# A sequence mixer and MLP on one core: transposes moved from TensorE to the DMA queue, part of the LayerNorm statistics from VectorE to ScalarE, and a new order of the tasks

## The chip, the core and the metric

One core of a Trainium2 chip runs the whole kernel in one launch. The metric is the device time of one execution in microseconds. Four runs of the kernel before gave 243.87, 244.04, 244.14 and 245.66, with a median of 244.09.

## What is computed

The inputs are bf16: `S` = 2048 rows of `D` = 512, and an MLP width of `F` = 1792. Cut to what matters:

```python
def A(q, k, v, shift_k, ssm_k, ssm_D):           # q is the LayerNorm of x = A_q
    k_shift = sum(k_pad[t:t+S] * shift_k[:, 3-t] for t in range(4))
    kv = k_shift * v
    y = causal_convolution(kv, ssm_k)             # by an FFT of length 2S
    return q * (y + kv * ssm_D)

def B(x, w1, w2, w3, w4):
    h  = gelu(layernorm(x) @ w1)
    hs = concat(h quarters shifted by -1, +1, -2, +2 rows) @ w2
    x1 = x + hs
    return x1 + gelu(layernorm(x1) @ w3) @ w4

h  = x + A(layernorm(x), ...)
h2 = h + B(layernorm(h), ...)
```

## The kernel before

The 2048 rows are held as 16 blocks of 128 rows by 512 columns, and most of the second half works on pairs of blocks (256 rows).

In the first half the long convolution is done as a discrete Fourier transform in two matmul steps each way. The names in the trace follow the steps: `nt` are transposes of k (L352), `pk` the short convolution (L371), `ph` and `pc` the first step for the filter and for the gated input (L326), `pg` and `pw` the second step (L404), `pv` the inverse second step (L490), and matmuls of L565 the inverse first step (tasks J and I, for four blocks at a time). Between the steps ScalarE (ACT) and VectorE (DVE) convert each PSUM tile to bf16 (`copy`, L265 on ACT and L267 on DVE), and DMAs on SP's queue rearrange it across partitions. The last of these DMAs is `ra<-rb` (L495), on which I waits. Two small groups of warm-up matmuls (`warm`, L509 to L512, 4 matmuls each) stand between the last inverse step and J; each waits for one of the last two conversions.

The second half goes block by block. A gate (L576, ACT, task Y) scales the inverse's PSUM tile into z. `hsum` (L585, DVE, task H) forms h from it, and `stats` takes its mean and variance by a bn_stats and a bn_aggr (L582, L583). For each pair `hvar` (DVE), `hnorm` (GpSimd, called POOL in the profile, with a power at L607) and `hbf` (any of three engines, L625 or L627, task hb) give the normalised bf16 block. `transposes` (L635 to L639) sends its four 128x128 tiles through TensorE (PE) by an identity matrix, and `tcopy` brings them from PSUM into `hnT`. Then follow `w1mm` (L653, task W(p, h): two for each pair), a gelu on ACT (L659, task U(p, h)), `w2mm` (L678, task X(b)), which reads the gelus of three neighbouring pairs because of the row shifts, `x1sum` on DVE (L683, task S, with its own `stats`), again a normalisation (`lbf`, task lb), four transposes and a copy into `lnT`, `w3mm` (L720, task M(g, f): 7 for each of 8 pairs), a gelu (L726), and `w4mm` (L735, task O(g, i): 14 matmuls for each of 16 blocks). `store` (L743, task Z) adds the residual and sends the block out on SP's queue; its tile has three buffers. Warm-up matmuls of L751 (4 for each of blocks 2 to 5) are strewn in; block 4's stands last of all PE work, behind the last O.

Which task is issued when is not left to a scheduler: `ORDER` is a list written out by hand or by a planner, of task numbers with the engine's letter (P for PE, A for ACT, V for DVE, G for POOL, D for a DMA on SP's queue). Each engine runs its tasks in this order, and SP's queue, which waits for a DMA's inputs before it issues it, does so too. The tasks' `opts` and `lat` are a planner's costs in microseconds; they no longer act at run time.

Of the kernel before, what the change touches and what calls it, by code (L numbers as in the profile page):

```python
# [34 lines left out]
7D 1D 2D 12G 69P 3D 67P 70A 68V 30P 4D 28P 31A 34P 29V 43P 6D 35A 37P 13G 44A 52P 38V 5D 48P 53A 46P 49V 0D 55P 47A 39P  # L35
41P 40V 56A 8D 65P 42A 66V 61P 59P 62V 63P 60V 57P 10D 64A 71P 58A 18G 14V 32P 75P 33A 9D 72V 25P 76V 19P 26A 79P 36D
276V 20A 277V 15A 21P 283V 73P 80V 22A 16V 23P 77P 74V 24A 280V 27D 89P 278V 50P 90A 83P 78V 51A 11D 297A 103P 84V 105P
81P 104A 281V 106A 275V 101P 82V 85P 279G 102A 282V 45D 111P 86V 284G 113P 112A 99P 100V 114A 125P 17G 123P 54D 126A
127P 124V 93P 128A 129P 94V 117P 130A 115P 108D 118A 91P 116V 131D 87P 92A 132D 137P 88V 141P 119D 138A 135P 107D 142V
139P 95D 136V 140A 97D 143P 157P 110D 144V 158V 153P 120D 147P 154A 134D 149P 148V 179P 121D 150A 151P 133D 180A 191P  # L40
152V 109D 185P 192A 96D 159P 181V 98D 173P 186A 155P 122D 160V 174A 182P 187V 156A 197P 161P 183A 193V 163P 198A 184D
188P 162V 164A 194P 199V 189A 203P 165P 204A 195V 209P 166A 205V 196D 200P 210A 215P 201A 206P 211V 216A 221P 202D 207V
167P 222A 190D 212P 217V 168A 208D 227P 175P 213A 223V 171P 228A 218P 176V 172A 233P 229V 219A 224P 214D 234A 239P 225V
220D 230P 240A 245P 235V 226D 231A 177P 169P 241V 246A 232D 236P 170A 251P 237V 178A 247V 252A 238D 242P 257P 253V 243A
248P 258A 263P 249V 254P 264A 244D 269P 259V 255A 250D 299D 270A 265V 260P 298D 271V 261A 266P 256D 285V 267A 272P 262D
288V 268D 295P 273A 291V 145P 290V 274D 296P 146A 292V 293V 303P 286V 294G 301D 287V 304P 305A 302G 289G 322A 306V 307A
325A 341P 308V 342P 323V 343A 309V 344V 362A 324P 310G 346A 326V 312G 379P 311G 315G 363V 313P 364A 380P 314A 316P 327P
400A 328V 347V 398A 329G 300D 317A 318P 349V 331G 365V 381A 334A 350G 348P 319A 366V 332P 399V 383A 335P 367G 355A 415P
401V 333A 369G 416P 372A 356P 320P 351G 336A 402V 368G 357V 417A 352V 373P 403G 370P 382V 419A 337P 374A 339P 371A 404G
# [12 lines left out]
679P 688A 660A 675P 682V 680A 673P 676A 631P 674A 681V 647P 632A 657P 648A 653P 658A 655P 654A 649P 656A 645P 650A 685P
646V 663P 686V 683P 664V 665P 684V 643P 666V 703P 644V 705P 704V 345P 706V
# [27 lines left out]
def kernel(  # L91
# [417 lines left out]
    def warm(e):  # L509
        pt = big(("wm",))  # L510
        for i in range(4):
            nc.tensor.matmul(pt[:, i % 2, :], lhsT=wup[:, 0:P], rhs=wup[:], start=True, stop=True)  # L512
# [71 lines left out]

    def hsum(b):  # L585
        def f(e):
            nc.vector.scalar_tensor_tensor(out=h_sb[:, b, :], in0=q_sb[:, b, :], scalar=qmv[:, b, 0:1], in1=tl["z", b][:],  # L587
                                           op0=SUB, op1=MUL)
            stats("hv", b, h_sb[:, b, :])
        return f  # L590
# [163 lines left out]
    for b in range(NB):  # L754
# [5 lines left out]
        if 1 < b < 6:  # L760
            task(("wm", b), {"PE": 0.87}, warm(b), [("H", b)], take="mm", rank=-100)
# [65 lines left out]
```

## Time and profile before

| | us |
|---|---|
| median of four runs | 244.09 |
| the profiled execution | 243.03 |
| its span, first to last instruction | 241.2 |
| PE busy | 222.3 (92%) |
| DVE busy | 158.3 (66%) |
| ACT busy | 135.6 (56%) |
| POOL busy | 53.2 (22%) |

A busy share is a mean over stages with different limits, so the stretches and the chain of waits say more than this table. In the rows of a group, the numbers behind the bar are its busy time, the mean duration of one in nanoseconds, and the idle time of the engine just before them with what ended it. Instructions of one engine overlap at their ends, so a dense run of them advances by busy time over count, a little less than the mean.

### The profile page before, as it was taken

The page shows a single profiled execution, that of the slowest core. Times are in us where ns is not written, and L with a number is a line of the kernel's source. Part 1 is how long each engine was busy: PE and PEld are TensorE (multiplying, and loading weights), DVE is VectorE, ACT ScalarE, POOL GpSimd, SP SyncE. Part 2 cuts the span into 40 slices and gives each one's busy share as a digit, 9 for nine tenths or more (in the row PEclk, how much of TensorE's full clock was granted, in tenths as well). Part 3 has the DMA queues.
Part 4 walks back from the last instruction along what each step waited for, and adds up shares of the span by engine and source line. Part 5 has one row for each costly group of instructions (what it writes and reads, how often), then busy time and mean ns, then how long its engine had stood idle before and what let it go on. Part 6 is the DMA issues. An engine that isn't in the chain of part 4 may idle for free.

```text
span 241.2 us, 4733 instructions
## 1 busy us (share of the span) xinstructions
PE 222.3 (92%) x1885; PEld 133.4 (55%) x1905; DVE 158.3 (66%) x324; ACT 135.6 (56%) x195; POOL 53.2 (22%) x102
## 2 busy tenths in 40 slices
PE   7879999798989956699999999999999999999995
PEld 3455454543332313369658757976565769864442
DVE  6686978999989969999998685147391253002221
ACT  3775697899999825689664333653014526730000
POOL 3760025000000052998715070001030000000000
PEclk9999999999999999799999999999999999999999
DMA  6998299881433999000000001000001000001111
GB/s 164 401 422 359 107 287 394 329 332 48 174 132 130 313 323 366 6 1 3 0 3 1 0 3 43 3 1 0 24 22 43 24 22 0 3 0 43 46 43 43
DMA packets 11816, 28.10 MB, mean 116 GB/s; under 512 B 1809, under 2 KB 6674, under 8 KB 10258
## 3 DMA queue, kind: packets, MB, share of 16 engines
q1 hardware_dynamic: 11264, 27.79, 31.1%
q8 instruction: 15, 0.25, 0.4%
q10 hardware_dynamic: 530, 0.01, 0.1%
q14 instruction: 7, 0.06, 0.1%
HBM read 13.11 MB, written 2.10 MB: 63 GB/s over the span
## 4 chain that ended last, share of the span: by engine, by line
PE 66%; DVE 12%; ACT 10%; DMA 6%; issue 4%; POOL 1%; SPq 1%; ACTq 0%; DVEq 0%; POOLq 0%
PE mm L720 20%; PE mm L735 20%; PE pk L371 6%; PE mm L678 5%; PE pv L490 4%; DMA ra<-in_A_ssm_k_dram 3%; PE mm L653 3%; DVE rb L267 2%; DMA ra<-rb 2%; PE ph L326 2%; DVE st L582 2%; ACT ra L265 2%; DVE rd L587 2%; ACT rb L265 2%; DVE rb L480 2%
## 5 line engine op out<-in xcount | busy, mean ns | idle before, releaser
L726 ACT ACTIVATE ra<-mm 128x512 bf16<-128x512 f32 x56 | 31.8, 600 | 36.6 <-PE mm L720 36.5
L720 PE MATMUL mm<-rc,rb 128*128 128x256 bf16 x448 | 52.0, 273 | 0.0
L735 PE MATMUL mm<-rt,ra 128*128 128x512 bf16 x218 | 49.3, 379 | 0.4
L720 PEld LDWEIGHTS <-rb 128*128 128x128 bf16 x448 | 43.5, 98 | 6.8
L743 DVE TENSOR_TENSOR ob<-mm,rd 128x512 bf16<-128x512 f32 x16 | 11.0, 688 | 42.3 <-PE mm L735 42.3
L735 PEld LDWEIGHTS <-ra 128*128 128x128 bf16 x224 | 21.9, 98 | 25.1
L490 PE MATMUL pv<-rb,rt 64*128 64x512 bf16 x128 | 17.0, 377 | 2.3 <-DVE rb L267 1.1
L265 ACT COPY rc<-ptx 128x512 bf16<-128x512 bf16 x21 | 12.0, 599 | 9.1 <-PE ptx L639 9.0
L371 PE MATMUL pk<-diag,rb 128*128 128x256 bf16 (+3 forms) x108 | 15.3, 285 | 1.2 <-ACT rb L265 1.0
L265 ACT CAST rb<-pw 128x1024 bf16<-128x1024 f32 x16 | 16.4, 1078 | 0.0
L683 DVE SCALAR_TENSOR_TENSOR q_sb<-rd,cr,mm 128x512 bf16<-128x512 bf16 x16 | 11.8, 735 | 6.9 <-PE mm L678 6.9
L653 PE MATMUL mm<-rc,rf 128*128 128x256 bf16 x128 | 16.1, 276 | 0.0
L678 PE MATMUL mm<-rf,rb 128*128 128x512 bf16 x57 | 15.5, 379 | 0.7 <-ACT rb L659 0.3
L607 POOL TENSOR_TENSOR r<-r,mhalf 128x2 f32<-128x2 f32 x8 | 6.2, 777 | 41.3 <-DVE xm L596 41.3
L456 POOL TENSOR_SCALAR qrs<-qmv 128x4 f32<-128x4 f32 x4 | 0.8, 194 | 64.6 <-DVE qmv L451 64.5
L265 ACT CAST rc<-ph 128x1024 bf16<-128x1024 f32 x12 | 11.7, 1027 | 4.4 <-PE ph L326 4.4
L576 ACT ACTIVATE z<-mm,qrs 128x512 f32<-128x512 f32 x16 | 10.4, 693 | 6.7 <-PE mm L565 4.5
L371 PEld LDWEIGHTS <-rb 128*128 128x128 bf16 x112 | 9.3, 98 | 8.5 <-issue 3.0
L653 PEld LDWEIGHTS <-rf 128*128 128x128 bf16 x128 | 12.5, 100 | 2.6 <-issue 0.6
L587 DVE SCALAR_TENSOR_TENSOR rd<-q_sb,qmv,z 128x512 bf16<-128x512 bf16 x16 | 12.0, 752 | 2.1 <-ACT z L576 2.1
L490 PEld LDWEIGHTS <-rt 64*128 64x128 bf16 x128 | 6.1, 94 | 12.8 <-issue 5.6
L267 DVE COPY rc<-ptx 128x512 bf16<-128x512 bf16 x11 | 4.4, 420 | 13.0 <-PE ptx L639 13.0
(129 smaller groups left out, 358.6 us busy)
## 6 DMA issues: line engine op xcount, KB each, us to landing
rd<-rc SPq DMA_DIRECT2D x16, 256.0 KB, 5.2
rc<-ra SPq DMA_DIRECT2D x16, 256.0 KB, 3.5
ra<-rb SPq DMA_DIRECT2D x16, 256.0 KB, 2.5
ra<-in_A_k_dram SPq DMA_DIRECT2D x4, 512.0 KB, 8.8
ra<-in_A_ssm_k_dram SPq DMA_DIRECT2D x4, 512.0 KB, 7.7
rb<-in_A_v_dram SPq DMA_DIRECT2D x2, 1024.0 KB, 12.6
q_sb<-in_A_q_dram SPq DMA_DIRECT2D x2, 1024.0 KB, 9.8
out_dram<-ob SPq DMA_DIRECT2D x16, 128.0 KB, 1.8
```

The costliest lines, as they stand in the source:

```text
L265: nc.scalar.copy(o, i)
L371: nc.tensor.matmul(pk[:, i, P * (m + lo):P * (m + hi + 1)], lhsT=kT[:, c, b, 2:P + 2] if b >= 0 else kT[:, c, NB + b, 1:P + 1], rhs=diag[: ...
L490: nc.tensor.matmul(ps[:, t, :], lhsT=tt[hs, min(x, 2), kh, :], rhs=pr[hs, x // 2, x % 2, :], start=(x == 0), stop=(x == 3))
L576: nc.scalar.activation(z[:], tl["y", b][:], ACT.Identity, bias=1.0, scale=qrs[:, b:b + 1])
L587: nc.vector.scalar_tensor_tensor(out=h_sb[:, b, :], in0=q_sb[:, b, :], scalar=qmv[:, b, 0:1], in1=tl["z", b][:], op0=SUB, op1=MUL)
L653: nc.tensor.matmul(pw_[:, j * 256:(j + 1) * 256], lhsT=w1_sb[:, k, m * P:(m + 1) * P], rhs=hnT[:, k, p * 256:(p + 1) * 256], start=(k == 0 ...
L678: nc.tensor.matmul(px[:], lhsT=shifted(m, b), rhs=w2_sb[:, m, :], start=(m == 0), stop=(m == DC - 1))
L683: nc.vector.scalar_tensor_tensor(out=x1[:, b, :], in0=hbm[:, b, :], scalar=tl["cr", b // 2][:, b % 2:b % 2 + 1], in1=tl["x", b][:], op0=MU ...
L720: nc.tensor.matmul(pg[:, j * 256:(j + 1) * 256], lhsT=w3_sb[:, k, fc * P:(fc + 1) * P], rhs=lnT[:, k, g * 256:(g + 1) * 256], start=(k == ...
L726: nc.scalar.activation(gbuf[:, g % 4, 2 * f:2 * f + 2, :], tl["g", g, f][:].rearrange("p (j x) -> p j x", j=2), ACT.Gelu_apprx_tanh)
L735: nc.tensor.matmul(po[:], lhsT=gbuf[:, g % 4, fc, i * P:(i + 1) * P], rhs=w4_sb[:, fc, :], start=(fc == 0), stop=(fc == FC - 1))
L743: nc.vector.tensor_tensor(out=ob[:], in0=tl["o", 2 * g + i][:], in1=xh1[:, b, :], op=ADD)
```

## The change

Five edits. First, pairs 4 to 7 of h (`HP = 4`) and all but the first two pairs of x1 (`LP = 2`) are no longer transposed by PE: each normalised block is stored to a scratch tensor in DRAM (`stored`), and when both blocks of a pair have landed, one DMA transposes them into `hnT` or `lnT` (`flipped`). PE's transposes and the copies from PSUM of these 20 blocks are gone, and SP's queue gets 20 stores of 128 KB and 10 transposing DMAs of 256 KB. Second, for pairs 0 to 2 of h (`HA = 3`) and pair 1 of x1 (`XA`), the mean comes from a sum that the scalar_tensor_tensor gives along with its result (`summed`), and the variance from a Square on ACT with an accumulated sum (`squares`, tasks Q and SQ) in place of bn_stats and bn_aggr. Third, the two groups of warm-ups ahead of J have 8 matmuls instead of 4. Fourth, the numbering shifts with the added and removed tasks. Fifth, `ORDER` is another list throughout, the first half included: on ACT it holds one conversion more of `pc` and one more of `pg`, two fewer of `nt`, one table eviction fewer, and the conversion of `f` ahead of the last `pv` rather than behind it; both warm-up groups stand behind the last `pv`; the w3 load precedes the w4 load; block 4's warm-up stands among the first W instead of last; and the first M stands behind 10 W and 4 X (before: 14 W and 7 X).

The diff, with the lists of numbers cut to their first lines:

```diff
--- before.py
+++ after.py
@@ -32,35 +32,35 @@
 KB = 1024
 
 ORDER = """
-7D 1D 2D 12G 69P 3D 67P 70A 68V 30P 4D 28P 31A 34P 29V 43P 6D 35A 37P 13G 44A 52P 38V 5D 48P 53A 46P 49V 0D 55P 47A 39P
...
+2D 3D 0D 12G 37P 5D 43P 38A 41P 44V 50P 7D 42A 46P 51A 48P 47V 4D 39P 18G 49A 52P 40V 1D 61P
...
 """
 
 class Plan:
@@ -508,7 +508,7 @@
             task(("qn", b // 4), {"G": 1.3}, qnorm(b - 3, b + 1), [("qs", c) for c in range(b - 3, b + 1)])
     def warm(e):
         pt = big(("wm",))
-        for i in range(4):
+        for i in range(8):
             nc.tensor.matmul(pt[:, i % 2, :], lhsT=wup[:, 0:P], rhs=wup[:], start=True, stop=True)
 
     for kh in range(NH - 2, NH):
@@ -534,7 +534,10 @@
     hbm = view(rd, NB * D, NB * D, "p (b d) -> p b d", b=NB)
     xh1, x1 = hbm, q_sb
 
+    HP, LP = 4, 2
+    HA, XA = 3, (1,)
     pools = {}
+    scr = ctx.enter_context(tc.tile_pool(name="scr", bufs=1, space=DRAM)).tile([2 * NB, P, D], BF16, name="scr")
 
     def mixer_pools():
         p0.close()
@@ -582,25 +585,43 @@
         nc.vector.bn_stats(st[:], src)
         nc.vector.bn_aggr(mv[:, b % 2, :], st[:])
 
+    def summed(name, b, src, early, **kw):
+        i = slice(b % 2, b % 2 + 1)
+        if early:
+            kw["accum_out"] = pair(name + "s", b // 2, 2, bufs=8)[:, i]
+        nc.vector.scalar_tensor_tensor(out=src, **kw)
+        if not early:
+            stats(name, b, src)
+
+    def squares(name, b, src):
+        def f(e):
+            i = slice(b % 2, b % 2 + 1)
+            jk = pools["ln"].tile([P, D], BF16, name="jk", tag="jk", bufs=2)
+            nc.scalar.activation(jk[:], src, ACT.Square, bias=pair(name + "s", b // 2, 2, bufs=8)[:, i], scale=-float(D),
+                                 accum_out=pair(name + "q", b // 2, 2, bufs=8)[:, i])
+        return f
+
     def hsum(b):
-        def f(e):
-            nc.vector.scalar_tensor_tensor(out=h_sb[:, b, :], in0=q_sb[:, b, :], scalar=qmv[:, b, 0:1], in1=tl["z", b][:],
-                                           op0=SUB, op1=MUL)
-            stats("hv", b, h_sb[:, b, :])
-        return f
+        return lambda e: summed("hv", b, h_sb[:, b, :], b // 2 < HA, in0=q_sb[:, b, :], scalar=qmv[:, b, 0:1], in1=tl["z", b][:],
+                                op0=SUB, op1=MUL)
 
     EPS = 1e-5
 
-    def negmean(p, n, mv):
+    def variance(name, p, early):
+        return (tl[name + "q", p][:], 1.0 / D ** 3) if early else (tl[name, p][:, :, 1], 1.0)
+
+    def negmean(p, n, name, early):
         nm = pair(n, p, 2, bufs=8)
-        nc.vector.tensor_scalar(out=nm[:], in0=mv[:, :, 0], scalar1=-1.0, scalar2=None, op0=MUL)
+        src, sc = (tl[name + "s", p][:], -1.0 / D) if early else (tl[name, p][:, :, 0], -1.0)
+        nc.vector.tensor_scalar(out=nm[:], in0=src, scalar1=sc, scalar2=None, op0=MUL)
 
     def hvar(p):
         def f(e):
             uw = pair("uw", p, 2, 2, bufs=8)
             for a, (m_, e_) in enumerate(((1.0, EPS), (1.0 + EPS, EPS * EPS))):
-                nc.vector.tensor_scalar(out=uw[:, a, :], in0=tl["hv", p][:, :, 1], scalar1=m_, scalar2=e_, op0=MUL, op1=ADD)
-            negmean(p, "hm", tl["hv", p])
+                src, sc = variance("hv", p, p < HA)
+                nc.vector.tensor_scalar(out=uw[:, a, :], in0=src, scalar1=m_ * sc, scalar2=e_, op0=MUL, op1=ADD)
+            negmean(p, "hm", "hv", p < HA)
         return f
 
     def power(out, in_, n):
@@ -642,6 +663,14 @@
     def tcopy(key, dstT, slot):
         def f(e):
             copy(e, dstT[:, :, slot * P:(slot + 1) * P], tl[("pt",) + key][:])
+        return f
+
+    def stored(key, slot):
+        return lambda e: nc.sync.dma_start(scr[slot], tl[key])
+
+    def flipped(dstT, scr_lo, n, lo):
+        def f(e):
+            nc.sync.dma_start_transpose(dstT[:, :, lo:lo + n * P], scr[scr_lo:scr_lo + n].rearrange("b p x -> (b p) x"))
         return f
 
     def w1mm(p, h):
@@ -679,16 +708,14 @@
         return f
 
     def x1sum(b):
-        def f(e):
-            nc.vector.scalar_tensor_tensor(out=x1[:, b, :], in0=hbm[:, b, :], scalar=tl["cr", b // 2][:, b % 2:b % 2 + 1],
-                                           in1=tl["x", b][:], op0=MUL, op1=ADD)
-            stats("xv", b, x1[:, b, :])
-        return f
+        return lambda e: summed("xv", b, x1[:, b, :], b // 2 in XA, in0=hbm[:, b, :], scalar=tl["cr", b // 2][:, b % 2:b % 2 + 1],
+                                in1=tl["x", b][:], op0=MUL, op1=ADD)
 
     def xvar(p):
         def f(e):
-            nc.vector.tensor_scalar(out=pair("r1", p, 2)[:], in0=tl["xv", p][:, :, 1], scalar1=1.0, scalar2=EPS, op0=MUL, op1=ADD)
-            negmean(p, "xm", tl["xv", p])
+            src, sc = variance("xv", p, p in XA)
+            nc.vector.tensor_scalar(out=pair("r1", p, 2)[:], in0=src, scalar1=sc, scalar2=EPS, op0=MUL, op1=ADD)
+            negmean(p, "xm", "xv", p in XA)
         return f
 
     def x1norm(p):
@@ -756,34 +783,50 @@
             T["J", b // 4] = plan.add({"PE": 1.32}, inv1(b // 4, range(6)), most + fet, "mm", 4)
             T["I", b // 4] = plan.add({"PE": 0.44}, inv1(b // 4, range(6, 8)), made + [T["J", b // 4]])
         task(("Y", b), {"A": 0.58}, gate(b), [("qn", b // 4), ("I", b // 4)], take="z", drop=("J", b // 4), part=b % 4)
-        task(("H", b), {"V": 1.63}, hsum(b), drop=("Y", b))
+        task(("H", b), {"V": 0.85 if b // 2 < HA else 1.63}, hsum(b), drop=("Y", b))
         if 1 < b < 6:
             task(("wm", b), {"PE": 0.87}, warm(b), [("H", b)], take="mm", rank=-100)
+        if b // 2 < HA:
+            task(("Q", b), {"A": 0.95}, squares("hv", b, h_sb[:, b, :]), [("H", b)])
         if b % 2:
             p = b // 2
-            task(("uw", p), {"V": 0.22}, hvar(p), [("H", b - 1), ("H", b)])
+            task(("uw", p), {"V": 0.22}, hvar(p), [("Q" if p < HA else "H", b - 1), ("Q" if p < HA else "H", b)])
             task(("rr", p), {"G": 1.55}, hnorm(p), [("uw", p)])
             task(("cr", p), {"G": 0.45}, hback(p), [("rr", p)])
             for c in (b - 1, b):
                 task(("hb", c), {"V": 0.34, "G": 0.9, "A": 0.72}, hbf(c), [("rr", p)])
-                task(("LT", c), {"PE": 0.24}, transposes(("hb", c)), [("hb", c)], take="pt")
-                task(("TE", c), {"A": 0.48, "V": 0.33}, tcopy(("hb", c), hnT, c), drop=("LT", c))
+                if p < HP:
+                    task(("LT", c), {"PE": 0.24}, transposes(("hb", c)), [("hb", c)], take="pt")
+                    task(("TE", c), {"A": 0.48, "V": 0.33}, tcopy(("hb", c), hnT, c), drop=("LT", c))
+                else:
+                    task(("LT", c), {"D": 0.5}, stored(("hb", c), NB + c), [("hb", c)], lat=LAND)
+            if p >= HP:
+                task(("TE", b), {"D": 2.4}, flipped(hnT, NB + b - 1, 2, (b - 1) * P), [("LT", b - 1), ("LT", b)], lat=5.0)
+                T["TE", b - 1] = T["TE", b]
             for h in range(2):
                 T["W", p, h] = plan.add({"PE": 0.87}, w1mm(p, h), [T["TE", b - 1], T["TE", b]] + w12t, "mm")
                 task(("U", p, h), {"A": 0.5}, w1gelu(p, h), drop=("W", p, h), deps=[("halo",)])
     for i, b in enumerate(order):
         need = {(b + o) % NB // 2: None for o in offs}
         task(("X", b), {"PE": 0.87}, w2mm(b), [("U", p, h) for p in need for h in range(2)], take="mm")
-        task(("S", b), {"V": 1.63}, x1sum(b), [("cr", b // 2)], drop=("X", b))
+        task(("S", b), {"V": 0.87 if b // 2 in XA else 1.63}, x1sum(b), [("cr", b // 2)], drop=("X", b))
+        if b // 2 in XA:
+            task(("SQ", b), {"A": 0.95}, squares("xv", b, x1[:, b, :]), [("S", b)])
         if i % 2:
             p = b // 2
-            task(("ux", p), {"V": 0.15}, xvar(p), [("S", b - 1), ("S", b)])
+            task(("ux", p), {"V": 0.15}, xvar(p), [("SQ" if p in XA else "S", b - 1), ("SQ" if p in XA else "S", b)])
             task(("r1", p), {"G": 1.15}, x1norm(p), [("ux", p)])
             for c in (b - 1, b):
                 task(("lb", c), {"V": 0.34, "G": 0.9, "A": 0.72}, lbf(c), [("r1", p)], take="lb")
-                task(("L", c), {"PE": 0.24}, transposes(("lb", c)), take="pt", drop=("lb", c))
-                task(("E", c), {"A": 0.48, "V": 0.33}, tcopy(("lb", c), lnT, order.index(c)), drop=("L", c),
-                     rank=400.0 - 20.0 * (order.index(c) // 2))
+                if i < 2 * LP:
+                    task(("L", c), {"PE": 0.24}, transposes(("lb", c)), take="pt", drop=("lb", c))
+                    task(("E", c), {"A": 0.48, "V": 0.33}, tcopy(("lb", c), lnT, order.index(c)), drop=("L", c),
+                         rank=400.0 - 20.0 * (order.index(c) // 2))
+                else:
+                    task(("L", c), {"D": 0.5}, stored(("lb", c), order.index(c)), drop=("lb", c), lat=LAND)
+            if i >= 2 * LP:
+                task(("E", b), {"D": 2.4}, flipped(lnT, i - 1, 2, (i - 1) * P), [("L", b - 1), ("L", b)], lat=5.0)
+                T["E", b - 1] = T["E", b]
     for g in range(NB // 2):
         bs = order[2 * g:2 * g + 2]
         for f in range(FC // 2):
```

More of the change, by code (lines that the diff above doesn't have):

```diff
@@ L40 @@
[L40 to L49, printed above, removed]
@@ new lines @@
+53A 59P 13G 62V 21P 6D 60V 67P 22A 23P 68V 55P 8D 24A 57P 56V 69P 58A 34P 70V 75P 35A 9D 63P 28P
+64V 71P 29A 76V 10D 14V 79P 45D 72V 15A 83P 80V 65P 297A 280V 11D 73P 84V 66A 16V 30P 19P 74V 54D 31A
+77P 276V 20A 277V 93P 87P 78V 94A 81P 88A 275V 281V 25P 89P 26A 82V 85P 17G 90A 283V 117P 86V 111P 27D 118A
+32P 33V 112A 129P 123P 130A 278V 127P 36D 125P 124A 128V 101P 126A 91P 102V 279G 105P 92A 113P 133D 106V 115P 114A 131D
+99P 116V 134D 103P 100A 95D 135P 282V 104A 96D 141P 139P 136V 119D 142A 284G 155P 107D 140V 137P 120D 156A 165P 110D 138V
@@ L64 @@
+628A 544D 675P 680V 641P 659V 679V 678A 660V 669P 676A 642V 673P 670A 649P 674A 665P 650A 653P 666A 697P 654A 685P 698A 699V
+695P 700V 686A 693P 696A 687P 694A 691P 688A 671P 692A 689P 672A 667P 690A 643P 668A 663P 644V 703P 664V 661P 704V 701P 662V
+683P 702V 681P 684V 682V
 """
```

38 lines of the change are left out of this document (20 added, 18 removed).

## The prediction

> **What bounds the kernel now.** I read the page's busy slices first, then the same by stretches of chosen length, then the chain that ended last, and only then the groups of instructions. The stretches, of which these five rows carry the argument:
>
> ```profile
> 50.00:60.00 10.00, 8.91 (x75) 3.83 (x70) 10.00 (x14) 10.00 (x12) 0.00 (x0) 1.00 0.46 187
> 95.00:100.00 5.00, 2.45 (x39) 1.29 (x29) 4.79 (x13) 2.26 (x4) 4.56 (x7) 0.91 0.24 94
> 100.00:105.00 5.00, 4.95 (x38) 2.83 (x41) 4.76 (x14) 3.99 (x7) 4.74 (x6) 0.75 0.01 2
> 110.00:115.00 5.00, 5.00 (x53) 4.41 (x52) 4.79 (x12) 4.97 (x10) 4.32 (x7) 1.00 0.01 3
> 140.00:150.00 10.00, 9.95 (x77) 6.75 (x77) 7.04 (x16) 3.57 (x7) 3.40 (x9) 1.00 0.08 28
> ```
>
> The columns of the table are PE, PEld, DVE, ACT, POOL, granted clock, DMA share. Three regimes: in the first third ACT and DVE evict PSUM at full load (10.00 of 10); from 89 to 102 DVE is full (4.79 of 5) and PE half idle (2.45), at a clock that sinks to 0.75; after that PE is full to the end. The chain shows the joints:
>
> ```profile
> 82.96 5.20 DMA ra<-rb
> 88.21 0.65 PE mm L565 x8
> 88.99 0.70 ACT z L576
> ...
> 117.39 1.75 PE mm L653 x16
> 119.14 0.86 PE mm L678 x4
> ...
> 127.29 1.75 PE mm L720 x16
> ...
> 129.90 3.49 PE mm L720 x32
> 133.39 0.22 PE ptx L639 x4
> ...
> 139.28 3.02 PE mm L735 x14
> ...
> 235.31 2.32 PE mm L735 x10
> 237.63 0.86 PE mm L751 x4
> ```
>
> This gives PE prices per task: 0.87 for W (L653, 8 matmuls) and M (L720, 3.49 for four), 0.86 for X, 3.02 for O (L735), 0.22 for one block's four transposes. A check that the last regime is nothing but PE: when the first M starts (127.29) the old order has 56 M, 16 O, 9 X, 2 W and 16 transposed blocks left, 48.9 + 48.3 + 7.7 + 1.7 + 3.5 = 110.1 us; the clock says 237.63 - 127.29 = 110.3. The warm-up behind the last O holds nothing up. So I forecast by one checkpoint: when the first M can start, and how much PE work is left then.
>
> **The change part by part.**
>
> *Transposes leave PE.* Eight blocks of h and twelve of x1 no longer pass PE: 20 x 0.22 = 4.4 us of the resource that sets the end. In the new order 56 M, 16 O, 12 X, 6 W and 2 transposed blocks follow the first M: 48.9 + 48.3 + 10.3 + 5.2 + 0.4 = 113.1 us.
>
> *Variances move from DVE to ACT.* These rows price the stretch before the first M (busy, mean of one; a dense run goes by busy over count):
>
> ```profile
> L576 ACT ACTIVATE z<-mm,qrs 128x512 f32<-128x512 f32 x16 | 10.4, 693 | 6.7 <-PE mm L565 4.5 <-DVE rd L587 1.5 <-issue 0.7
> L265 ACT COPY rc<-ptx 128x512 bf16<-128x512 bf16 x21 | 12.0, 599 | 9.1 <-PE ptx L639 9.0
> L659 ACT ACTIVATE rb<-mm 128x512 bf16<-128x512 f32 x16 | 9.7, 627 | 5.4 <-PE mm L653 2.9 <-PE mm L678 2.5
> L625 ACT ACTIVATE rd<-rd,hm,rr 128x512 bf16<-128x512 bf16 x4 | 3.3, 813 | 5.4 <-POOL hm L613 5.2
> L582 DVE BATCH_NORM_STATS2 st<-rd 128x6 f32<-128x512 bf16 x16 | 11.1, 695 | 0.5
> L583 DVE BATCH_NORM_AGGREGATE hv<-st 128x2 f32<-128x6 f32 x16 | 2.9, 182 | 0.5
> ```
>
> Each of the six early h blocks (and two x1 blocks) takes 0.70 + 0.18 off DVE and puts a Square with an accumulated sum on ACT; the sum that rides on the scalar_tensor_tensor has no row. The Square's bounds: 0.60 (the gelu) to 1.28 (dearest, a table load, below); the nearest row is L625, bf16 in and out with a pointer bias, 0.81; I take 0.90 for the extra result. DVE gains about 8 x 0.8 = 6.4 us there, but ACT becomes the limit. Counting the new order on ACT from the first gate (88.99) to U(3,0): 16 gates x 0.65, 7 copies x 0.57, 8 gelus x 0.61, 3 normalisations x 0.81, 8 Squares x 0.90 = 10.4 + 4.0 + 4.9 + 2.4 + 7.2 = 28.9, so 117.9 without any wait. Behind it stand X4 and X5 on PE (they read U(3,0)), two transposed blocks and ACT's two copies: 1.72 + 0.44 + 1.14, and some 0.3 of hand-overs: the first M at 121.5. The last O then ends at 121.5 + 113.1 = 234.6 where it was 237.63: -3.0 us. So the front gives back 1.4 of the 4.4.
>
> *The detour through DRAM.* A pair (blocks 8 and 9 first) is stored twice 128 KB, then one DMA transposes 256 KB into place. The trace has no transposing DMA; like-sized and larger ones:
>
> ```profile
> rd<-rc SPq DMA_DIRECT2D x16, 256.0 KB, 5.2
> ra<-rb SPq DMA_DIRECT2D x16, 256.0 KB, 2.5
> ra<-in_A_k_dram SPq DMA_DIRECT2D x4, 512.0 KB, 8.8
> rb<-in_A_v_dram SPq DMA_DIRECT2D x2, 1024.0 KB, 12.6
> out_dram<-ob SPq DMA_DIRECT2D x16, 128.0 KB, 1.8
> ```
>
> By ACT's count hb9 is ready after 12 gates, 6 Squares, 5 copies, 4 gelus and 2 normalisations: 88.99 + 7.8 + 5.4 + 2.9 + 2.4 + 1.6 = 109.1. Store 1.8, issue 0.5: the transpose starts at 111.4. W(4) is wanted at 118.0 - 1.74 = 116.3, ahead of X4. So the transpose is free up to 4.9 us. Bounds 2.5 to 12.6; I take 5.0, near the slower row of its own size: nothing. Were the cover gone, each further us of it would be a us of PE. On SP the transpose waits for its stores, and the next stores, the output stores of Z among them, queue behind that wait; the output tiles have three buffers, and later consumers lie further off (W(6) 8.9 us of PE behind the first M, M(2) 23.0, W(7) 26.5), so 0.
>
> [...]
>
> *Warm-ups.* Two groups grow from 4 to 8 matmuls, both now after the last eviction:
>
> ```profile
> 83.31 1.04 PE L512 MATMUL wm<-wup 128*128 128x512 bf16 x4
> 83.59 1.28 SPq L273 DMA_DIRECT2D rt<-in_B_w_dram  x1
> 86.44 2.59 PE L565 MATMUL mm<-ra,f 32*128 32x512 bf16 x34 [2.10 <-DMA ra<-rb]
> ```
>
> 16 x 0.22 = 3.5 from 83.3 ends at 86.8, 0.4 after the first inverse matmul could start; but its last data lands only at 88.21, so 0 (bounds +0.4; and -0.5, should the clock of 0.75 at 100 to 105 rise to 1). The w3 load (which waits for the same landing) now precedes w4's: the last return may land up to 2.7 sooner (5.2 against the median 2.5), hidden by the warm-ups; w3 and w4 are wanted after 121, so 0.
>
> *The order up to 82 us.* The same evictions, dealt otherwise. On ACT one conversion more of pc and of pg, two fewer of k's transposes, one table eviction fewer, and f's before the last product instead of after it:
>
> ```profile
> L265 ACT CAST ra<-pc 128x1024 bf16<-128x1024 f32 x11 | 10.4, 1031 | 3.2 <-PE pc L326 3.2
> L265 ACT CAST rd<-pg 128x1024 bf16<-128x1024 f32 x10 | 10.2, 1062 | 0.7 <-PE pg L404 0.7
> L265 ACT COPY rb<-nt 128x1024 bf16<-128x1024 bf16 x4 | 4.0, 1027 | 2.5 <-DVE rb L267 1.5 <-PE nt L352 1.0
> L265 ACT COPY rt<-tb 128x512 bf16<-128x512 bf16 x4 | 2.3, 676 | 0.0
> L422 ACT ACTIVATE rt<-tb 128x512 bf16<-128x512 bf16 x2 | 1.4, 708 | 0.0
> L265 ACT CAST f<-f 128x1024 bf16<-128x1024 f32 x1 | 1.0, 1012 | 0.5 <-PE f L437 0.5
> ```
>
> 1.03 + 1.06 - 2.05 - (2 x 0.68 + 0.71) + 1.01 = -1.0 us on an engine that is busy 10.00 of 10 (50 to 60 us). I take -0.8, bounds -2 to +2, since a new order can open waits that no row shows.
>
> **Sum.** -3.0 - 0.8 = -3.8. The profiled execution took 243.03 (span 241.2 and 1.8 around it), so 239.2 by its own time. It lies 1.1 below the median of the four runs, 244.09, which the comparison is made with: 240.3. About 0.5%, 1.2 us, is what a measurement of this kernel can tell from no change.
>
> **The rivals.**
>
> *ACT does not bind.* If the Squares run near 0.6 and hide in ACT's gaps (it is busy 2.26 of 5 at 95 to 100), PE's chain alone counts. First gate 88.99, four gates 2.6, two Squares 1.2, then from the statistics to the first normalised block 2.7 by
>
> ```profile
> 94.48 0.20 DVE L602 TENSOR_SCALAR uw<-hv 128x2 f32<-128x2 f32 x2
> 94.76 1.51 POOL L607 TENSOR_TENSOR rr<-uw,mhalf 128x4 f32<-128x4 f32 x1 [5.42 <-DVE hm L596]
> 97.16 0.76 POOL L627 TENSOR_SCALAR rd<-rd,rr,hm 128x512 bf16<-128x512 bf16 x1
> ```
>
> and 2 for normalising, transposing, copying: W starts at 97.5, with hand-overs 98.3; PE is full today only from some 101 on. From there 16 W, 16 X, 56 M, 16 O, 10 blocks, the last inverse (32 matmuls, by the row of 34 in 2.59) and a warm-up: 13.9 + 13.8 + 48.9 + 48.3 + 2.2 + 2.4 + 0.9 = 130.4, ending at 228.7 against 237.63, -8.9: 235.2; with a quarter of that given back, 237.4. For it: DVE's load in the profile. Against: ACT at 4.97 of 5 from 110 to 115 already, with 7.2 us more to do.
>
> *Squares reload tables.* The profile has two table loads, the second for the gelu,
>
> ```profile
> L516 ACT ACT_TABLE_LOAD x1 | 1.3, 1283 | 0.0
> ```
>
> and none between gate, copy and gelu; Square is new. In the new order it would swap four times ahead of U(3,0): +5.1, 245.4; with two swaps 242.9. [...]
>
> *The transposing DMA is slow: slower than before.* Taken one after another at 8.8 us (the 512 KB row): the first lands at 120.2, 3.9 late for W(4), and the first M slips to 125.4; the third lands at 111.4 + 26.4 = 137.8, wanted by W(6) at 125.4 + 8.9 = 134.3, 3.5 late; the fifth at 155.4, for W(7) just in time. 240.3 + 7.4 = 247.7. At 12.6 the three are 7.7, 11.1 and 7.6 late: near 266. The sign turns at about 7.6 us a pair (2.7 and 1.1 late). For it: rows are turned into columns of 2-byte values on the way, which no transfer of the trace does. Against: DMA engines are idle from 100 us on (share 0.01), and only three of the ten transfers have a near consumer.
>
> **How the numbers follow.** My case (237.5 to 243) 0.52, of which 0.05 is within 0.5% of 244.09; ACT not binding (235.0 to 237.5) 0.21; tables (242.9 to 245.4) 0.08, 0.05 of it as same; slow transposes 0.19, all slower. Faster 0.47 + 0.21 = 0.68; same 0.10; slower 0.19 + 0.03 = 0.22. The range leaves the slow transposes out: 235.0 to 245.4. Faster holds most of the chance, so my case's own range stands above.
>
> **What would show it.** Right: first L720 near 121, ACT without gaps from 89 to 118, PE at 9.95 of 10 after it, transposing DMAs landing within some 5 us, the last O ending near 234. Wrong: PE idle before L653 or L720 with a DMA as releaser (slow transposes); table loads beside the Squares; gaps in ACT while PE starts W at 98 (the first rival); the first gate later than 89 (the order up to 82).

## The result

The changed kernel takes 236.08 us (median of 11 runs, 235.79 to 238.62) against 243.87 us (median of 15): the ratio is 0.9705, with a 95% interval of 0.9674 to 0.9736. It is faster by 2.9%, about twice the 1.6% that was forecast; 236.08 lies inside the range of 235.0 to 245.4, below my own case's 237.5 to 243. The profiled execution took 236.02 us with a span of 234.2, so 7.0 us of span are gone where 3.8 were forecast. Some executions run slow, longer at a lower granted clock (in changed_again 239.90 and 241.22 us at 0.993 and 0.986, the others 236.22 to 236.56 at 0.997 to 1.00); the ratios leave them out, and of the profiles read below those of stats_on_dve and squares_twice are such executions.

The same stretches as before, of the changed kernel (PE, PEld, DVE, ACT, POOL, granted clock, DMA share):

```profile
95.00:100.00 5.00, 4.95 (x58) 2.83 (x58) 4.86 (x16) 5.00 (x12) 3.93 (x6) 1.00 0.76 246
100.00:105.00 5.00, 5.00 (x66) 3.50 (x65) 4.79 (x15) 4.96 (x9) 4.04 (x10) 1.00 0.02 3
110.00:115.00 5.00, 4.60 (x33) 2.76 (x30) 4.29 (x14) 2.59 (x7) 4.50 (x13) 1.00 0.35 101
115.00:120.00 5.00, 4.11 (x39) 3.36 (x39) 4.76 (x12) 3.21 (x6) 0.69 (x1) 1.00 0.53 119
120.00:125.00 5.00, 4.50 (x36) 3.10 (x35) 3.71 (x12) 2.40 (x5) 4.42 (x8) 1.00 0.16 45
140.00:150.00 10.00, 9.95 (x82) 7.82 (x81) 5.66 (x11) 4.57 (x9) 0.00 (x0) 1.00 0.04 13
```

Before, PE was half idle from 95 to 100, and its clock was 0.91 and then 0.75 up to 105; now PE, DVE and ACT are all full there and the clock is 1.00. PE has short gaps until 125 and hardly any later (9.95 of 10 from 140 to 150). The marks of the chain, and the row in which the first M starts:

```profile
81.29 4.96 DMA ra<-rb
86.29 0.61 PE mm L568 x8
...
87.70 0.70 ACT z L579
...
220.81 10.11 PE mm L762 x46
230.94 0.69 DVE ob L770
```

```profile
116.81 4.53 PE L747 MATMUL mm<-rc,rb 128*128 128x256 bf16 x40 [0.67 <-ACT rc L265]
```

The first gate comes at 87.70 (before: 88.99), the first M at 116.81 (127.13), the last O ends at 230.9 (237.63). The prediction set 88.2, 120.7 and 233.8, its 0.8 us for the first half taken off its marks. Counted by its own sections, forecast against measured: to the first gate 88.2 and 87.7; from there to the first M 32.5 and 29.1; from there to the last O's end 113.1 and 114.1; behind it 3.6 and 3.3. **The surprise is one section, between the first gate and the first M: 3.4 us.** Another 0.8 of the difference is that the median of before in 15 runs lies 0.84 above its profiled execution, while the changed kernel's lies 0.06 above.

The two new operations, first the Squares on ACT and then the detour's rows:

```profile
89.99 0.74 ACT L600 ACTIVATE jk<-rd,hvs 128x512 bf16<-128x512 bf16 x1
...
90.61 0.21 ACT L600 ACTIVATION_READ_ACCUMULATOR jk<-rd,hvs 128x1 f32 x1
90.70 0.73 ACT L600 ACTIVATE jk<-rd,hvs 128x512 bf16<-128x512 bf16 x1
...
91.31 0.21 ACT L600 ACTIVATION_READ_ACCUMULATOR jk<-rd,hvs 128x1 f32 x1
91.40 0.70 ACT L579 ACTIVATE z<-mm,qrs 128x512 f32<-128x512 f32 x1
```

```profile
scr<-rd SPq DMA_DIRECT2D x8, 128.0 KB, 1.8
rc<-scr SPq DMA_TRANSPOSE x10, 3.3
```

```profile
107.82 1.34 SPq L673 DMA_TRANSPOSE rc<-scr  x1
...
111.18 1.92 PE L682 MATMUL mm<-rc,rf 128*128 128x256 bf16 x16 [0.27 <-DMA rc<-scr]
```

A Square and its accumulator read (the 128x1 row behind it) last 0.74 and 0.21, but the next Square starts 0.71 behind the first: two of them advance ACT by 1.41, not by the 1.8 that the prediction counted. The transposing DMA lands 3.3 us after its issue; for the first pair it lands just as W(4) wants it, and PE waits 0.27.

### The profile page after: what moved, and what is told of

It reads as the page before. It is cut to its first block, busy times and chain, and to the rows that moved or that the text cites. A ratio compares the mean times of both kernels' runs of the same rounds, so it can differ in the third digit from the quotient of the medians.

```text
span 234.2 us, 4619 instructions
## 1 busy us (share of the span) xinstructions
PE 219.7 (94%) x1815; PEld 127.5 (54%) x1833; DVE 148.5 (63%) x310; ACT 132.6 (57%) x193; POOL 57.1 (24%) x106
## 2 busy tenths in 40 slices
DMA packets 25255, 33.33 MB, mean 142 GB/s; under 512 B 12689, under 2 KB 20114, under 8 KB 23698
## 4 chain that ended last, share of the span: by engine, by line
PE 67%; DVE 15%; DMA 4%; POOL 4%; issue 4%; ACT 4%; ACTq 0%; POOLq 0%
PE mm L762 21%; PE mm L747 19%; PE pv L490 7%; PE pk L371 6%; DVE rd L592 4%; PE mm L707 4%; DVE st L585 3%; PE pw L404 3%; DMA ssk_bf<-in_A_shift_k_dram 2%; PE mm L682 2%; DMA ra<-rb 2%; ACT rb L265 2%; PE ph L326 1%; DVE ra L267 1%; PE pc L326 1%
## 5 line engine op out<-in xcount | busy, mean ns | idle before, releaser
L753 ACT ACTIVATE ra<-mm 128x512 bf16<-128x512 f32 x56 | 32.5, 597 | 40.9 <-PE mm L747 40.9
L747 PE MATMUL mm<-rc,rb 128*128 128x256 bf16 x448 | 50.9, 273 | 0.7 <-ACT rc L265 0.7
L628 POOL TENSOR_TENSOR r<-r,mhalf 128x2 f32<-128x2 f32 x8 | 7.1, 884 | 44.0 <-DVE xm L616 44.0
L371 PE MATMUL pk<-diag,rb 128*128 128x256 bf16 (+3 forms) x108 | 14.8, 285 | 0.4 <-ACT rb L265 0.2
L682 PEld LDWEIGHTS <-rf 128*128 128x128 bf16 x128 | 12.3, 98 | 3.4 <-DMA rc<-scr 0.5
L579 ACT ACTIVATE z<-mm,qrs 128x512 f32<-128x512 f32 x16 | 10.1, 694 | 5.6 <-PE mm L568 5.5
L265 ACT CAST ra<-pc 128x1024 bf16<-128x1024 f32 x12 | 11.6, 1018 | 2.0 <-PE pc L326 1.8
L326 PEld LDWEIGHTS <-f 128*32 128x32 bf16 x256 | 6.5, 98 | 10.8 <-issue 5.8
L404 PEld LDWEIGHTS <-rf 128*64 128x64 bf16 x128 | 6.2, 108 | 10.5 <-issue 7.0
L737 DVE SCALAR_TENSOR_TENSOR rd<-q_sb,qmv,rd 128x512 bf16<-128x512 bf16 x16 | 11.8, 768 | 0.0
```

The lines of the kernel that those rows point to most:

```text
L265: nc.scalar.copy(o, i)
L326: nc.tensor.matmul(ps[32 * bq:32 * bq + 32, t, :], lhsT=f1[:, h, t, :], rhs=xs(bq), start=True, stop=True)
L371: nc.tensor.matmul(pk[:, i, P * (m + lo):P * (m + hi + 1)], lhsT=kT[:, c, b, 2:P + 2] if b >= 0 else kT[:, c, NB + b, 1:P + 1], rhs=diag[: ...
L404: nc.tensor.matmul(ps[64 * t:64 * t + 64, r, :], lhsT=ftab[:, kh, r, t, :], rhs=z[:, kh, t, :], start=True, stop=True)
L682: nc.tensor.matmul(pw_[:, j * 256:(j + 1) * 256], lhsT=w1_sb[:, k, m * P:(m + 1) * P], rhs=hnT[:, k, p * 256:(p + 1) * 256], start=(k == 0 ...
L737: nc.vector.scalar_tensor_tensor(out=xh1[:, b, :], in0=x1[:, b, :], scalar=qmv[:, b, 0:1], in1=h_sb[:, b, :], op0=ADD, op1=ADD)
```

## The experiments

All ratios are to the kernel before, with 95% intervals. The first gate comes at different times even in kernels whose first half is the same (the changed kernel, changed_again, pe_transposes, no_strewn_warmups, transpose_twice, stats_on_dve, squares_twice, front_trimmed): from 87.7 to 91.2 us in the profiled executions. So the profiles are compared from the first gate on, and one gate alone says little. The table collects them; the last four columns are us, the last three from the first gate to the first W, the first M, and the end of the last O.

| kernel | ratio | gate | W | M | last O |
|---|---|---|---|---|---|
| before | 1 | 89.0 | 12.8 | 38.1 | 148.6 |
| changed | 0.9705 [0.9674, 0.9736] | 87.7 | 10.1 | 29.1 | 143.2 |
| changed_again | 0.9654 [0.9591, 0.9716] | 87.8 | 10.1 | 29.3 | 143.3 |
| pe_transposes | 0.9895 [0.9827, 0.9963] | 88.0 | 10.1 | 29.6 | 147.7 |
| stats_on_dve | 0.9995 [0.9950, 1.0040] | 91.2 | 14.1 | 35.7 | 150.9 |
| order_alone | 1.0105 [1.0047, 1.0164] | 88.3 | 13.2 | 35.8 | 153.8 |
| squares_alone | 1.0040 [0.9994, 1.0086] | 88.5 | 14.9 | 39.7 | 150.2 |
| detour_alone | 1.0076 [1.0031, 1.0120] | 90.8 | 12.3 | 41.8 | 150.5 |
| squares_twice | 0.9948 [0.9897, 0.9998] | 91.0 | 15.5 | 35.1 | 148.8 |
| no_strewn_warmups | 0.9684 [0.9585, 0.9784] | 88.0 | 9.2 | 29.3 | 143.3 |
| transpose_twice | 0.9887 [0.9836, 0.9938] | 89.6 | 10.1 | 33.2 | 148.1 |
| old_first_half | 0.9729 [0.9688, 0.9770] | 89.4 | 10.1 | 29.3 | 143.4 |
| four_warmups | 0.9708 [0.9646, 0.9770] | 89.6 | 11.4 | 30.6 | 144.7 |
| front_trimmed | 0.9664 [0.9601, 0.9727] | 90.8 | 10.1 | 28.6 | 142.2 |

The theory going in was the prediction's, with its size put right: ACT sets the pace up to the first M, PE from there on. The rivals: PE's own queue sets the front; the new order carries the gain by itself; the detour is the critical piece.

### pe_transposes: the transposes back on PE

```diff
-    HP, LP = 4, 2
+    HP, LP = 8, 8
 # ORDER: in the place of each transposing DMA, L(b) and L(b+1) on PE, E(b) on ACT, E(b+1) on DVE; no stores
```

> The changed kernel with all 32 blocks transposed by TensorE again (four transposes and one copy a block, half of the copies on ACT and half on DVE, at the place of the transposing DMA in the order); everything else as changed. Theory (20 x 0.22 us taken off TensorE, which sets the end once the first M runs): 236.1 + 4.4 = 240.5 us, 239.5 to 241.5, TensorE 4.4 us busier. Rival (the gain came from the new order and the shorter statistics, and the detour through DRAM costs as much in waits as it saves): 236 to 238.

The median was 241.6, within the theory's range. In its chain the last O ends at 235.73, 147.7 from the first gate:

```profile
88.01 0.69 ACT z L580
...
215.00 20.73 PE mm L763 x96
```

That is 4.5 more than the changed kernel's 143.2, for 20 x 0.22 = 4.4 counted. The ratios agree: 0.9895 - 0.9705 = 1.9%, 4.6 us. The first M comes only 0.5 later. So the transposes cost their full PE time, and they cost it behind the first M.

### stats_on_dve: the statistics back on DVE

```diff
-    HA, XA = 3, (1,)
+    HA, XA = 0, ()
 # ORDER: the eight Squares taken out
```

> The changed kernel with every mean and variance from bn_stats and bn_aggr on DVE again and no Squares on ACT; order otherwise as changed. Theory of the prediction (what DVE gains there ACT loses, so the move is worth 1 us at most): 236 to 237. Rival (DVE is the slower of the two from the first gate on, 8 x 0.8 = 6.4 us come back in front of the first M): first M 4 to 6 us later, 240 to 242.

The median was 243.58, beyond the rival's range and far from the theory's: the whole gain is gone (0.9995). Counted from the gate, W comes 4.1 and the first M 6.6 later, about the 8 x 0.8 = 6.4 added on DVE, and the last O 7.7; the medians differ by 7.5. The clock falls too: it is 0.65 from 95 to 100, where PE is busy 2.53 of 5, and 0.66 up to 105, where the changed kernel has 1.00:

```profile
95.00:100.00 5.00, 2.53 (x7) 0.88 (x7) 4.78 (x13) 2.12 (x4) 1.44 (x1) 0.65 1.06 378
100.00:105.00 5.00, 5.00 (x46) 2.05 (x45) 4.63 (x14) 0.99 (x2) 2.81 (x7) 0.66 0.46 143
```

DVE is full (4.78 and 4.63 of 5) while ACT stands at 2.12 and 0.99. My belief that ACT loses what DVE gains was wrong as a statement of worth: without the Squares ACT idles in front of a full DVE.

### squares_twice and no_strewn_warmups: which engine sets the front with the change in place

```diff
-            nc.scalar.activation(jk[:], src, ACT.Square, ...)
+            for _ in range(2):
+                nc.scalar.activation(jk[:], src, ACT.Square, ...)
```

> The changed kernel with each of the eight Squares done twice (the second writes the same values): 8 x 0.71 = 5.7 us more on ACT. Theory (ACT, busy 4.97 of 5 us until 110, sets when U(3,0) and the first M come): first M 4 to 5.7 us later than 116.8, time 240 to 242. Rival (TensorE's own queue sets the front, ACT's load is hidden): within 1 us of 236.1.

The median was 243.68; by the ratio it is 0.9948 x 243.87 = 242.6, just above the theory's range. From the gate the first M comes 6.0 later and the last O 5.6, for 5.7 added to ACT; the ratios differ by 2.4%, 5.9 us. Two stretches of it show ACT at 4.90 and 4.94 of 5, with PE waiting in the first and its clock at 0.50 in the second:

```profile
95.00:100.00 5.00, 1.84 (x11) 0.70 (x9) 2.23 (x7) 4.90 (x12) 1.55 (x4) 0.95 1.06 378
100.00:105.00 5.00, 4.09 (x37) 1.45 (x38) 3.96 (x12) 4.94 (x13) 3.04 (x3) 0.50 0.42 133
```

```diff
-        if 1 < b < 6:
+        if 1 < b < 4:
             task(("wm", b), {"PE": 0.87}, warm(b), [("H", b)], take="mm", rank=-100)
```

> The changed kernel without the warm-up matmuls of blocks 4 and 5, which stand among the first W (2 x 0.87 us of TensorE at 96.9 and 99.1 us). Theory (ACT sets the front): 235.6 to 236.6, the first M where it was. Rival (TensorE sets the front): 234.4 to 235.3, the first M 0.9 to 1.7 us earlier.

The median was 236.61. The first W starts 0.9 earlier, the first M and the last O where they were (29.3 and 143.3, as in changed_again). PE was full only with warm-ups: without them it shows gaps, and nothing comes sooner.

```profile
95.00:100.00 5.00, 4.61 (x60) 2.99 (x61) 4.90 (x14) 5.00 (x11) 3.96 (x5) 1.00 0.83 266
100.00:105.00 5.00, 4.37 (x59) 2.85 (x58) 4.79 (x15) 5.00 (x11) 4.12 (x9) 1.00 0.00 0
```

So PE does not set the front of the changed kernel. ACT has no room for more work there, and by stats_on_dve neither has DVE. Which of the two comes last can be read from the changed kernel's own trace. ACT hardly waits from the first gate to 110, and then it waits for DVE; the chain that ended last runs over DVE from 92.13 to 110.1, and it reaches PE for good only behind the first M, at the transposes of 124.39:

```profile
110.90 0.72 ACT L600 ACTIVATE jk<-q_sb,xvs 128x512 bf16<-128x512 bf16 x1 [0.80 <-DVE q_sb L592]
```

```profile
92.13 0.76 DVE rd L592
...
109.77 0.35 DVE uw L623 x2
110.27 0.20 POOL cr L641
...
124.39 0.40 PE ptx L660 x4
```

So the two are level within a microsecond, with DVE the later by 0.80 at that point. No run takes work off one of them alone, so what relieving ACT, or DVE, by itself would bring is not shown. The first rival had W right (97.5 to 98.3; it starts at 97.75), but its mechanism falls: it let PE alone count and the Squares hide in ACT's gaps, and there are hardly any while they run. That its time of 235.2 was nearest is luck.

### squares_alone, detour_alone, order_alone: each edit by itself

```diff
 # squares_alone: old ORDER, each Square directly behind its H or S; HP, LP = 8, 8; 4 warm-ups
 # detour_alone:  old ORDER, each store directly behind its hb or lb; HA, XA = 0, (); 4 warm-ups
 # order_alone:   new ORDER as in pe_transposes, without Squares; HP, LP = 8, 8; HA, XA = 0, ()
```

> The kernel before with one edit alone: sums on the scalar_tensor_tensor and Squares on ACT for pairs 0 to 2 of h and pair 1 of x1, each Square directly behind its block's sum in the old order; all transposes on TensorE, 4 warm-ups. Theory (both engines are near full from the first gate to the first M, so 6.4 us off DVE against 5.7 on ACT gains little unless the order is rebuilt around it): 241.5 to 244. Rival (DVE alone was the limit, the edit carries the gain by itself): 237 to 239.5.

> The kernel before with one edit alone: the 20 blocks go through DRAM, each store directly behind its normalisation and the transposing DMA behind the second store; statistics on DVE, old order, 4 warm-ups. In the old order W(5) and W(4) follow their normalisation within 2 us, while store and transpose take 1.8 + 3.3 us and more. Theory (the 4.5 us come only if the order hides the detour): TensorE waits 3 us or more at W(5) and W(4), 241.5 to 246. Rival (TensorE's time is the limit whatever the order): 239 to 240.

> The changed kernel with both replaced operations undone: all transposes on TensorE, all statistics on DVE, in the new order with 8 warm-ups a group. Theory (the order was built around the two edits and is worth nothing without them: undoing the transposes alone cost 5.5, undoing the statistics alone 7.5): 244 to 250. Rival (the new order by itself carries a part of the gain): 238 to 242.

None of the three is faster; the medians were 246.19, 246.59 and 247.15, on chips where the kernel before had 244.59, 244.59 and 245.00. By the ratios they are 244.8, 245.7 and 246.4: the theories of a dear detour and of a worthless order held in time, and squares_alone came out above its theory's range, which its interval still touches. In the old order, with each Square directly behind its sum, DVE waits for ACT's gates and Squares. In squares_alone (us waited in all, how many times, the longest):

```profile
DVE rd L593 <- ACT z L580: 5.0, 4, 1.8
DVE uw L624 <- ACT jk L601: 3.4, 2, 3.2
```

```profile
90.00:95.00 5.00, 3.35 (x35) 1.17 (x29) 2.40 (x8) 4.05 (x9) 1.57 (x2) 0.98 1.06 391
95.00:100.00 5.00, 3.43 (x29) 1.30 (x32) 3.25 (x12) 3.38 (x8) 4.43 (x6) 0.50 0.21 79
```

DVE, 4.80 and 4.79 of 5 before, falls to 2.40 and 3.25: it was unloaded and then made to wait. Another place for the Squares in the old order was not tried. In detour_alone W(5) stands right behind its normalisation, and PE waits for the DMA in this row; the theory expected as much at W(4) too, but no other W waits for these DMAs, and PE's waits for them elsewhere come to less than 2.2 us in all:

```profile
118.63 1.37 PE L683 MATMUL mm<-rc,rf 128*128 128x256 bf16 x8 [3.03 <-DMA rc<-scr]
```

In the new order the four combinations go 1.0105 with neither edit, 0.9995 with the detour, 0.9895 with the Squares, 0.9705 with both. The Squares are worth 2.1% and 2.9%, the detour 1.1% and 1.9%. That each is worth more with the other is not shown: the 0.8% is no more than the intervals of the four allow. The order alone loses 1.1%, and without it neither edit gains as placed here; both edits together in the old order were not tried.

### transpose_twice: how much slack the detour has

```diff
+            for _ in range(2):
-            nc.sync.dma_start_transpose(...)
+                nc.sync.dma_start_transpose(...)
```

> The changed kernel with each of the ten transposing DMAs issued twice in a row (the second writes the same values), so that each pair is ready 1.2 to 3.3 us later. Theory (only the first pair has no slack: W(4) started as its data landed; the others have some microseconds): 0.7 to 2 us slower, 236.8 to 238. Rival 1 (all are hidden with room): within 0.5 of 236.1. Rival 2 (several are at their edge): 3 us or more slower.

The median was 242.01, worse than the theory. A pair takes 6.4 us from its first issue to W(4), 3.1 more: two issues to the same place hold the queue for 4.43, where a single one takes 1.23 to 1.34 and two in a row to different places, in the changed kernel, 2.58; so the second seems to wait for the first.

```profile
109.69 4.43 SPq L674 DMA_TRANSPOSE rc<-scr  x2
...
116.05 2.61 PE L683 MATMUL mm<-rc,rf 128*128 128x256 bf16 x16 [3.29 <-DMA rc<-scr]
```

About 3.1 us more on the DMA give a wait of 3.29 at W(4) instead of 0.27; the clock falls behind it (0.71 from 115 to 120), and the 16 matmuls take 2.61 instead of 1.92. The first M comes 4.1 later and the last O 4.9. Only two later rows wait for a transposing DMA, by half a microsecond each:

```profile
150.02 1.05 PE L683 MATMUL mm<-rc,rf 128*128 128x256 bf16 x8 [0.52 <-DMA rc<-scr]
...
177.59 8.03 PE L748 MATMUL mm<-rc,rb 128*128 128x256 bf16 x72 [0.55 <-DMA rc<-scr]
```

So the first pair alone is at its edge, as the theory had it. The time falls into the range of the second rival, but by the size of the delay and the clock, not by several pairs at their edge.

### old_first_half and four_warmups: what lies ahead of the first gate

```diff
 # old_first_half: the first half's tasks in ORDER's same slots, in the old sequence
 # four_warmups:
-        for i in range(8):
+        for i in range(4):
             nc.tensor.matmul(pt[:, i % 2, :], lhsT=wup[:, 0:P], rhs=wup[:], start=True, stop=True)
```

> The changed kernel with the tasks of the first half (up to the loads of w3 and w4 and the last warm-ups) in their old sequence. Theory (the first gate came 1.3 us earlier by the new sequence: 87.70 against 88.99): 237.4, 236.7 to 238.3. Rival (the first half plays no part): 235.7 to 236.5.

> The changed kernel with 4 matmuls in each of the two warm-up groups ahead of J, as before. Theory of the prediction (worth nothing): 235.6 to 236.6. Rival (TensorE's clock falls while it waits from 82 to 86 us and the first matmuls of J, W and the warm-ups run at a lower clock, as at 95 to 105 before): clock below 0.95 in some stretch from 85 to 105 and 236.8 to 239.

old_first_half gave 237.76, inside its theory's range: the first gate at 89.36, 1.7 later, and everything behind it unchanged. But gates differ by more than that between kernels with the same first half, and the intervals of its ratio and the changed kernel's overlap, so this is not clear of noise. four_warmups gave 237.41, and its profile shows what the rival described:

```profile
85.79 4.02 PE L568 MATMUL mm<-ra,f 32*128 32x512 bf16 x34 [2.99 <-DMA ra<-rb]
```

```profile
85.00:90.00 5.00, 4.02 (x34) 1.35 (x35) 1.41 (x4) 0.44 (x1) 2.40 (x4) 0.50 0.41 108
90.00:95.00 5.00, 4.69 (x31) 1.56 (x32) 3.09 (x11) 3.82 (x9) 1.19 (x3) 0.51 1.02 401
```

PE waits 2.99 us ahead of J, the clock falls to 0.50, and 34 matmuls of J take 4.02 us instead of 2.69; the gate comes 1.9 later, the last O another 1.4. This execution, of 239.34 us at a mean clock of 0.978, is the longest of the four; the others took 236.50, 237.32 and 237.50 at 0.998, 0.993 and 0.991. So the 1.9 is the dear case, the median is 1.0 above changed_again's 236.45, and the intervals of the two ratios overlap: the profile shows the mechanism, the time does not show its worth. In the kernel before, the wait at the same place was 2.10 us and the clock stayed at 1.00 from 85 to 90: the conversion table's matmuls (L437, 0.63 us from 82.75) stood between its warm-ups. The new order moved them away, and the longer warm-ups stand in the hole. The old order is not safe either: in detour_alone, with the old first half, PE waits 3.2 us there and the clock is 0.50 from 90 to 95. The length of one wait is not all of it: in the kernel before, the clock sank to 0.75 from 100 to 105 with no wait of PE behind the gate longer than 1.76.

### front_trimmed and changed_again

```diff
-    HP, LP = 4, 2
+    HP, LP = 4, 1
 # ORDER: ux1, r1(1), lb3, lb2 (now on DVE) ahead of H15 and hb12; X5 behind L2; W(6,0) and U(6,0) behind O(0,0)
```

> The changed kernel with six moves: blocks 4 and 5 of x1 go through DRAM too (two transposed blocks less, 0.4 us of TensorE); the statistics of x1's first pair, its power and both normalisations go ahead of H(15) on DVE and of POOL's hb(12), the second one on DVE; X(5) stands behind the two transposes instead of ahead of them; W(6,0) stands directly behind O(0,0). Theory (the first M waits for this chain, 115.7 us at its last transpose): first M 0.5 to 0.8 us earlier after the gate, time 235.2 to 235.8. Rival (TensorE's later short waits take it back): 235.9 to 236.6.

> The changed kernel itself, as the yardstick on the same chip: 236.1, 235.7 to 236.6.

The medians were 237.59 and 236.45. From the gate the first M of front_trimmed comes 0.6 earlier and the last O 1.0 earlier than in the changed kernel, as the theory had it:

```profile
119.34 4.53 PE L748 MATMUL mm<-rc,rb 128*128 128x256 bf16 x40
```

By the ratio its time is 235.7, inside the forecast, but by the same measure the changed kernel has 235.4 on that chip: the ratios, 0.9664 and 0.9654, are not told apart. Whether it is the faster version stays open.

## Why the prediction missed the size

**Right: what bounds the end.** PE prices by task gave 113.1 us behind the first M; it took 114.1; of the 1.0 more, 0.45 is one wait for `lb` at 124.39. The transposes' 4.4 us were measured as 4.5 (pe_transposes).

**Half right: ACT binds in front of the first M.** squares_twice passes its added time on in full, and no_strewn_warmups moves nothing. But DVE, which the prediction took to be relieved, is as full: stats_on_dve passes its added time on too, and where ACT first waits, by 0.80, it waits for DVE.

**Wrong: ACT's pace, the term that was mis-sized.** The prediction let ACT need 28.9 us from the first gate to U(3,0). It needed 25.7 (87.70 to 113.39), 0.8 of it the wait for DVE. That is 3.2 of the 3.4 us by which the first M came earlier than forecast. By the distance from each start to the next in the changed kernel's timeline:

| on ACT, gate to U(3,0) | forecast | measured |
|---|---|---|
| 16 gates | 10.4 | 9.4 |
| 7 copies | 4.0 | 3.3 |
| 8 gelus | 4.9 | 4.0 |
| 3 normalisations | 2.4 | 2.4 |
| 8 Squares | 7.2 | 5.8 |
| wait for DVE | 0 | 0.8 |
| sum | 28.9 | 25.7 |

The new instruction is the smaller part: the Squares were 1.4 too dear, the gates, copies and gelus, which the old kernel has too, 2.6. They were priced by busy time over count, but each begins before its predecessor ends. Four gates in a row last 2.43 us in the changed kernel, 0.61 each, and yet start 0.57 apart (87.70 to 89.99), since the last one's full length is counted in; in shorter runs it counts for more. The kernel before showed the same distances, in rows that the prediction did not use:

```profile
104.46 0.81 ACT L625 ACTIVATE rd<-rd,hm,rr 128x512 bf16<-128x512 bf16 x1
105.17 0.56 ACT L265 COPY rc<-ptx 128x512 bf16<-128x512 bf16 x1
...
109.32 0.64 ACT L659 ACTIVATE rb<-mm 128x512 bf16<-128x512 f32 x1
109.81 0.72 ACT L576 ACTIVATE z<-mm,qrs 128x512 f32<-128x512 f32 x1
110.38 0.63 ACT L265 COPY rc<-ptx 128x512 bf16<-128x512 bf16 x1
110.84 0.67 ACT L659 ACTIVATE rb<-mm 128x512 bf16<-128x512 f32 x1
```

A gelu advances ACT by 0.49, a gate by 0.57, a copy by 0.46, and L625, the row next to the Square, by 0.71, not by its duration of 0.81. With 0.71 for the Square as well, an estimate from these rows is 24.1 for the whole count, against 24.9 measured without the wait. The Square advances ACT by the same 0.71; the accumulator read hides at the joint with the next instruction (90.61 to 90.82, the next Square from 90.70), so nothing had to be added for the sum.

**Not shown in size: the warm-ups at nothing.** Their cover was named, the last landing at 88.21, but the clock was treated as a bound of -0.5. The profile of four_warmups has 1.9 at the gate, in the longest of its executions; the median is 1.0 above changed_again's. The prediction's -0.8 for the first half was near the 1.3 by which the gate came earlier, but one gate is no measure (87.7 to 91.2), and neither old_first_half nor four_warmups is clear of noise.

**Half right: the detour.** It lands in 3.3 us, under the 5.0 taken and the 4.9 allowed, and costs 0.27 at W(4). ACT was 4 us ahead of its forecast there (the store's issue at 105.0 instead of 109.1), and the transpose was issued at 107.82 instead of 111.4; but PE was free for W(4) at 110.9 instead of 116.3, so 3.1 us were allowed and not 4.9. That the cover held was a near thing. transpose_twice confirms that a further us of DMA is a us of PE, and more by the clock: 3.1 us of DMA give 3.0 of waiting, and at a clock of 0.71 W(4)'s matmuls take 0.69 longer. The slow rival falls: its sign turned at about 7.6 us a pair, and the row has 3.3; the plain 256 KB transfers of this trace land in 2.4 to 5.7.

**Fallen: table loads.** The changed kernel has the same two ACT_TABLE_LOADs of 1.28 us as before, at 1.71 and 22.59 (before: 1.72 and 31.59); a Square between gates and gelus brought none.

**A gap in the reasoning.** The prediction added edits up: transposes off PE, statistics moved, order changed. The runs show that no edit gains alone. The order loses 1.1% without them, and each of them loses or gains nothing in the old order as placed there. That the order has to make room for both was seen for the detour but not for the Squares.

## What to carry to other kernels

Price a dense run of one engine by the distance between starts in the timeline, not by durations or busy time over count (a gate here: 0.57, against 0.69 and 0.65); price a new instruction by the same measure of its nearest row, and put the doubt into the range. Where two engines are both near full in a stretch, as ACT and DVE here, moving work between them paid only with an order that kept them from waiting for each other (the Squares: 2.1% and 2.9% in the new order, nothing in the old, at 1.0040); judge such an edit together with its order. When instructions that keep TensorE busy are moved out of a wait, look at how long the wait becomes: here the granted clock fell to 0.50 behind a wait of 2.99 us in one execution.

## What the runs showed of the hardware

The sum that rides on a scalar_tensor_tensor shows on DVE as an instruction of its own of 0.08 us (`DVE_READ_ACCUMULATOR`), and such operations in a row started 0.67 us apart. A transposing DMA holds SP's queue for 1.23 to 1.34 us at its issue, where a plain store takes 0.33 to 0.52. It moves 256 KB in many small packets: the kernel's packets rose from 11816 to 25255, those under 512 B from 1809 to 12689, and ten more such DMAs in transpose_twice brought 10560 more, all under 512 B; in the changed kernel it still landed in 3.2 to 3.8 us. A Square between gates and gelus brought no table load: both of the changed kernel's start before 23 us, the first gate at 87.70. At the wait ahead of J, TensorE's clock stayed at 1.00 over 2.10 us (before) and fell to 0.50 behind 2.99 (four_warmups) and 3.2 (detour_alone).
